# One transfer over 128 partitions in place of two of 64, in a gated convolution and MLP kernel

## The chip, the cores and the metric

The kernel runs on one core of a Trainium2 chip. The metric is the device time of one execution, in microseconds (us). A profiled execution gives a page and a trace, in which the engines are PE (TensorE), DVE (VectorE), ACT (ScalarE), POOL (GpSimd) and SP (SyncE, which here issues nearly all DMAs).

## The reference

2048 rows of 640 channels go through two branches, which a gate mixes row by row.

```python
x = A_q                                        # [1, 2048, 640], bfloat16
g = sigmoid((x * gate_w).sum(-1, keepdims=True))
# branch A: short convolution of k, product with v, long convolution along the rows
kv = conv4(A_k, A_shift_k) * A_v
y  = long_conv(kv, A_ssm_k) + kv * A_ssm_D     # by FFT of length 4096 along the rows
a  = x * y
# branch B: an MLP whose hidden channels are shifted by +1, -1, +2, -2 rows, and a second MLP
h  = gelu(layernorm(x) @ w1)
x1 = x + shift(h) @ w2
b  = x1 + gelu(layernorm(x1) @ w3) @ w4        # w3: 640 x 1536
out = g * a + (1 - g) * b
```

## The kernel before

**Layout of the rows.** A row number is split as 32n + 16g + s, with n from 0 to 63, g (the group) 0 or 1 and s from 0 to 15. Row (n, g, s) lies on partition 64g + n, in slot s of that partition. So one partition holds 16 slots of 640 bfloat16 values (1280 bytes), and in DRAM consecutive n of one group are 32 rows apart, while the two groups are 16 rows apart. The helper `tok` makes the DRAM view:

```python
def tok(ap):
    return ap.rearrange("(n g s) c -> g n s c", g=2, s=16)
```

**Moving rows.** x, k, v, a second reading of q and the output are moved in chunks of two or four slots of all 128 partitions. Since the view has the group as its first index, the kernel uses a helper, `halves` (L377 to L383; its issues stand as L382 in the profile), which issues two transfers one behind the other on SP's queue, of 64 partitions each, group 1 first:

```python
def fn(t):
    for g in (1, 0):
        nc.sync.dma_start(out=out(t, g), in_=in_(t, g))
```

It is called for x (`ldx`, 2 or 4 slots, tile `x`), for k (`ldk`, 4 slots, tile `K`), for v (`ldv`, 4 slots, tile `VC`), for q (`ldq`, 2 slots, tile `QO`) and for the first 12 slots of the output (`st`, 2 slots, from tile `QO`). The last four slots of the output (L1059) are stored slot by slot, half on SP's queue and half on ACT's. Weights, the spectra on their way through DRAM (`FH`, `FXD`, `GD` and back by `FX`, `GX`) and the transposed activations (`x1nT`, `XB`, by DMA transpose, L808) are moved by transfers of their own.

**Order.** The program is a list of tasks whose order is written out by hand (`ORDER`); each engine runs its tasks in that order, and so does SP's queue. A planner (`Plan.place`) turns that list into buffers. A transfer waits on SP's queue until its data or its buffer is ready, and for the transfer eight before it, whose semaphore it takes over.

**Stages.** First x comes in slot by slot (`ldx`), is normalised, transposed and multiplied with w1 (PE L689, L693). Then the products with w2 follow (PE L715), with the first step of the transform of the filter (PE L911) between them. Meanwhile DVE makes kv in four groups `gi` of four slots, from 3 to 0: four products (L878) and three sums (L882), then one product with v (L886, `fin`). There is one buffer for v, so that `ldv` of a group waits for the `fin` of the group before. The first step of the transform of kv (PE L913) writes `FXD`; after all of it `FX` is read back, and PE runs the second step (L965), the product of spectra (DVE L980) and the way back (L993) beside w3 (L817) and w4 (L833). At the end the last step (PE L1031) is scaled by gate and q (DVE L1037), the MLP branch is added (L1064, or L1045 and L1051 for the last four slots), and the output is stored. There are two buffers for q and two for the output, of two slots each.

Of the kernel before, what the change touches and what calls it, by code (L numbers as in the profile page):

```python
# [16 lines left out]
P = 128  # L17
D = 640
# [7 lines left out]
HALF = 1.27  # L26
# [328 lines left out]
def build(env, nc, io):  # L355
    pl = Plan()
    add = pl.add
# [3 lines left out]
    BF = 2  # L361
# [6 lines left out]
    if io:  # L368
# [4 lines left out]
        qv, kv_, vv, ov = tok(q2), tok(k2), tok(v2), tok(o2)  # L373
# [1 line left out]
    def dma(name, nbytes, fn, issue=0.58, **kw):  # L375
        return add(name, "SP", issue, fn, nbytes=nbytes, **kw)

    def halves(name, nbytes, out, in_, **kw):

        def fn(t):  # L380
            for g in (1, 0):
                nc.sync.dma_start(out=out(t, g), in_=in_(t, g))  # L382
        return add(name, "SP", 1.08, fn, nbytes=nbytes, **kw)  # L383

    def copy(t, out, in_):
        if t.on == "ACT":
# [26 lines left out]
    def c_ones(t):  # L413
# [6 lines left out]
        w=[("K", "z")], roles=("K",))  # L420
# [80 lines left out]
    def c_bm(t):  # L501
        for g in range(2):
# [8 lines left out]
                                                  in_=io["sk"].rearrange("d j -> (d j)").unsqueeze(0)), w=["CJR"], roles=("VC",))  # L511
# [25 lines left out]


    for s0, n in ((2, 2), (4, 2), (6, 4), (0, 2), (14, 2), (10, 4)):
        halves(f"ldx{s0}", P * n * D * BF * (HALF if n < 4 else 1.05), lambda t, g, s0=s0, n=n: env["x"][64 * g:64 * g + 64, s0:s0 + n, :],  # L540
               lambda t, g, s0=s0, n=n: qv[g, :, s0:s0 + n, :], w=[("x", s, g) for s in range(s0, s0 + n) for g in range(2)])
    dma("ldw1", 819200, lambda t: nc.sync.dma_start(out=env["W12"][:, 0], in_=io["w1"].rearrange("(t p) n -> p t n", p=P)),
        w=["W1"], roles=("W12",))
    dma("ldw2a", 655360, lambda t: nc.sync.dma_start(out=env["W12"][:, 1, 0:4, :],
# [7 lines left out]
        dma(f"ldsk{cb}", 524288, lambda t, cb=cb: nc.sync.dma_start(out=env["SK"][:, cb, :], in_=io["h"][128 * cb:128 * cb + 128, :]),  # L552
            w=[("SK", cb)], roles=("SK",))
    for i0 in (15, 11, 7, 3):
        halves(f"ldk{i0}", P * 4 * D * BF * 1.05, lambda t, g, i0=i0: env["K"][64 * g:64 * g + 64, i0:i0 + 4, :],
               lambda t, g, i0=i0: kv_[g, :, i0 - 3:i0 + 1, :], w=[("K", i, g) for i in range(i0, i0 + 4) for g in range(2)], roles=("K",))
    dma("ldkh1", 64 * 3 * D * BF * HALF, lambda t: nc.sync.dma_start(out=env["K"][64:128, 0:3, :], in_=kv_[0, :, 13:16, :]),
        w=[("K", i, 1) for i in range(3)], roles=("K",))

# [308 lines left out]


    for gi in (3, 2, 1, 0):  # L870
        halves(f"ldv{gi}", P * 4 * D * BF * 1.05, lambda t, g: env["VC"][64 * g:64 * g + 64, 0, :, :],
               lambda t, g, gi=gi: vv[g, :, 4 * gi:4 * gi + 4, :], w=["V"], roles=("VC",))
        a = 4 * gi

        def tap(t, j, o, a=a):
            VC = env["VC"]
            w = VC[:, 3, j:j + 1, :].broadcast_to([P, 4, D])
            nc.vector.tensor_tensor(out=VC[:, o], in0=env["K"][:, a + 3 - j:a + 7 - j, :], in1=w, op=ALU.mult)  # L878

        def acc(t):  # L880
            VC = env["VC"]
            nc.vector.tensor_tensor(out=VC[:, 1], in0=VC[:, 1], in1=VC[:, 2], op=ALU.add)  # L882

        def fin(t, a=a):
            VC = env["VC"]
            nc.vector.tensor_tensor(out=env["K"][:, a + 3:a + 7, :], in0=VC[:, 1], in1=VC[:, 0], op=ALU.mult)  # L886
        for j in (3, 2, 1, 0):
            rk = [("K", i, g) for i in range(a + 3 - j, a + 7 - j) for g in range(2)] + ([("K", "z")] if a + 3 - j < 3 else [])
            add(f"kv{gi}.m{j}", "DVE", 1.485, lambda t, j=j, a=a: tap(t, j, 1 if j == 3 else 2, a), r=rk + [("CJ", j)],
                w=["VA" if j == 3 else "VB"], roles=("K", "VC"))  # L890
            if j < 3:
                add(f"kv{gi}.a{j}", "DVE", 1.485, acc, r=["VB"], w=["VA"], roles=("VC",))
        add(f"kv{gi}.v", "DVE", 1.49, fin, r=["VA", "V"], w=[("K", i, g) for i in range(a + 3, a + 7) for g in range(2)] +
            [("kv", s) for s in range(a, a + 4)], roles=("K", "VC"))
# [121 lines left out]
    for s0 in range(0, 16, 2):  # L1016
        def rg(t, s0=s0):
            src = env.G.rearrange("k (x n) c -> (k x) (n c)", n=32)[:, 1280 * s0:1280 * s0 + 2560]
            nc.sync.dma_start(out=env["GX"][:, t.buf["GX"][0], :], in_=src)
        ld = dma(f"rG.{s0}", P * 5120, rg, issue=0.5, r=[("G", m) for m in range(10)], acq=("GX",), after=("FX",))  # L1020
        qown = halves(f"ldq.{s0}", P * 2 * D * BF * 1.3, lambda t, g: env["QO"][64 * g:64 * g + 64, 2 * t.buf["Q"][0]:2 * t.buf["Q"][0] + 2, :],
                      lambda t, g, s0=s0: qv[g, :, s0:s0 + 2, :], acq=("Q",), w=[("q", s0)], after=("W12",))
        oown = None
        for i in range(2):
            s = s0 + i

            def mm(t, s=s, i=i, ld=ld):
                X = env["GX"][:, ld.buf["GX"][0], :]
                for (c0, c1) in ((0, 512), (512, 640)):
                    for g in range(2):  # L1030
                        nc.tensor.matmul(env.Uf(t.buf["U"][0])[64 * g:64 * g + 64, c0:c1], lhsT=env["BT"][:, s, 64 * g:64 * g + 64],  # L1031
                                         rhs=X[:, 1280 * i + 640 * g + c0:1280 * i + 640 * g + c1], start=True, stop=True)
            t = add(f"s4.{s}", "PE", 0.29, mm, use=[ld], r=["BT"], rel=[(ld, "GX")], acq=("U",), mode="c64")

            def yq(t_, s=s, i=i, q=qown, t=t):
                u = env["W4"][:, 12 + t_.buf["V"][0], :]
                nc.vector.scalar_tensor_tensor(out=u, in0=env.Uf(t.buf["U"][0])[:, 0:D], scalar=SS("GG")[:, s:s + 1],  # L1037
                                               in1=env["QO"][:, 2 * q.buf["Q"][0] + i, :], op0=ALU.mult, op1=ALU.mult)
            y = add(f"yq.{s}", "DVE", 0.88, yq, use=[t], rel=[(t, "U"), (qown, "Q")], r=["GG", ("q", s0)], acq=("V",),
                    after=("C0",))  # L1040

            if s in LATE:
                def ax(t_, s=s, y=y):
                    u = env["W4"][:, 12 + y.buf["V"][0], :]
                    nc.vector.scalar_tensor_tensor(out=u, in0=env["x"][:, s, :], scalar=SS("OG")[:, s:s + 1], in1=u, op0=ALU.mult, op1=ALU.add)  # L1045
                a = add(f"ax.{s}", "DVE", 0.88, ax, use=[y], r=["GG", ("x", s, 0), ("x", s, 1)])
                for n, (c0, c1) in enumerate(((0, 512), (512, 640))):
                    w = late[s, n]

                    def fo(t_, s=s, i=i, y=y, o=oown, w=w, c0=c0, c1=c1):  # L1050
                        nc.vector.scalar_tensor_tensor(out=env["QO"][:, 4 + 2 * (o or t_).buf["O"][0] + i, c0:c1],  # L1051
                                                       in0=env.PS[:, w.buf["U"][0], 0:c1 - c0], scalar=SS("OG")[:, s:s + 1],
                                                       in1=env["W4"][:, 12 + y.buf["V"][0], c0:c1], op0=ALU.mult, op1=ALU.add)
                    o = add(f"fo.{s}.{n}", "DVE", (0.74, 0.27)[n], fo, use=[a, w] + ([oown] if oown else []), rel=[(y, "V"), (w, "U")],
                            w=[("o", s, n)], after=("W12",), **(dict(acq=("O",)) if oown is None else {}))
                    oown = oown or o
                def st(t, s=s, o=oown, i=i):
                    for g, q in ((1, nc.sync), (0, nc.scalar)):
                        q.dma_start(out=ov[g, :, s, :], in_=env["QO"][64 * g:64 * g + 64, 4 + 2 * o.buf["O"][0] + i, :])  # L1059
                add(f"st.{s}", "SP", 0.58, st, nbytes=P * D * BF * 1.3, r=[("o", s, 0), ("o", s, 1)], rel=[(oown, "O")])  # L1060
                continue

            def ad(t_, s=s, i=i, y=y, o=oown):
                nc.vector.scalar_tensor_tensor(out=env["QO"][:, 4 + 2 * (o or t_).buf["O"][0] + i, :], in0=env["x"][:, s, :],  # L1064
                                               scalar=SS("OG")[:, s:s + 1], in1=env["W4"][:, 12 + y.buf["V"][0], :], op0=ALU.mult, op1=ALU.add)
            kw = dict(acq=("O",)) if oown is None else {}
            o = add(f"ad.{s}", "DVE", 0.88, ad, use=[y] + ([oown] if oown else []), rel=[(y, "V")], r=["GG", ("x", s, 0), ("x", s, 1)],
                    w=[("o", s)], after=("W12",), **kw)
            oown = oown or o
        if s0 in LATE:  # L1070
            continue
        halves(f"st.{s0}", P * 2 * D * BF * 1.3, lambda t, g, s0=s0: ov[g, :, s0:s0 + 2, :],
               lambda t, g, o=oown: env["QO"][64 * g:64 * g + 64, 4 + 2 * o.buf["O"][0]:6 + 2 * o.buf["O"][0], :],
               r=[("o", s0), ("o", s0 + 1)], rel=[(oown, "O")])
    pl.close()
    return pl
# [30 lines left out]
```

## Time and profile before

| | |
|---|---|
| median of 3 runs | 225.56 us (224.49 to 228.49) |
| profiled execution, its own time | 227.05 us |
| its span, first to last instruction | 225.3 us |
| PE busy | 212.7 us (94%) |
| DVE busy | 189.3 us (84%) |
| ACT busy | 154.4 us (69%) |
| moved by DMA | 57.94 MB, mean 257 GB/s |

Busy times are unions over the span. A DMA view lists the issues by tile: how many, how many KB each (1 KB is 1024 bytes), and the median time from issue to landing. A view by windows gives, for a stretch of time, each engine's busy time, the granted clock of PE, the busy share of the core's 16 DMA engines and what they moved in GB/s (10^9 bytes). The chain is the work that ended last, followed back from the last instruction to what released each step.

### The profile page before, as it was taken

How to read it: one execution, taken by the hardware profiler on the slowest of the kernel's cores; microseconds unless marked ns; L12 is line 12 of the kernel's file. 1: busy time of each engine (PE TensorE's matmuls, PEld its weight loads, DVE VectorE, ACT ScalarE, POOL GpSimd, SP SyncE). 2: the span in 40 equal slices, each digit the busy share in tenths (PEclk: the TensorE clock that was granted, in tenths of full speed). 3: DMA queues.
4: the chain of work that ended last, by engine and by line, in shares of the span. 5: the costliest groups of instructions: out<-in, count | busy, mean ns of one | idle time of the engine just before them, and what ended most of it. 6: DMA issues, size and time to landing. Idle time of an engine off the chain costs nothing.

```text
span 225.3 us, 5381 instructions
## 1 busy us (share of the span) xinstructions
PE 212.7 (94%) x2161; PEld 106.4 (47%) x2178; DVE 189.3 (84%) x281; ACT 154.4 (69%) x225; POOL 45.8 (20%) x86
## 2 busy tenths in 40 slices
PE   3999889899999999999999999999999999999992
PEld 1576454466444444345543433334444555555561
DVE  7998896999999999997469989899857426989984
ACT  6998969799988999889658988888675002225000
POOL 7481532436200009930710000000000000000000
PEclk9999999999999999999999999999999999999999
DMA  6999999999999998979899989999992596988624
GB/s 193 281 308 232 220 237 238 327 233 327 349 240 287 241 272 252 379 270 270 193 367 311 373 154 285 316 304 309 247 255 88 185 374 209 281 250 249 203 64 116
DMA packets 39503, 57.94 MB, mean 257 GB/s; under 512 B 15027, under 2 KB 30645, under 8 KB 39478
## 3 DMA queue, kind: packets, MB, share of 16 engines
q1 hardware_dynamic: 39158, 57.27, 89.9%
q10 hardware_dynamic: 320, 0.33, 0.5%
q8 instruction: 17, 0.28, 0.5%
q14 instruction: 8, 0.07, 0.1%
HBM read 35.56 MB, written 18.36 MB: 239 GB/s over the span
## 4 chain that ended last, share of the span: by engine, by line
PE 63%; DMA 17%; DVE 12%; SPq 3%; issue 2%; ACT 1%; DVEq 0%
PE PS L817 18%; PE PS L833 17%; PE PS L715 9%; DMA x<-in_A_q_dram 7%; PE PS L965 5%; DMA W<-in_B_w_dram 4%; PE PS L689 4%; PE PS L993 4%; DMA SK<-in_A_ssm_k_dram 3%; DVE VC L878 3%; DVE VC L882 3%; DMA QO<-in_A_q_dram 2%; SPq L382 2%; PE PS L911 2%; PE PS L1031 1%
## 5 line engine op out<-in xcount | busy, mean ns | idle before, releaser
L824 ACT ACTIVATE h2T<-PS 128x512 bf16<-128x512 f32 x48 | 27.9, 605 | 27.3 <-PE PS L817 26.9
L833 PE MATMUL PS<-W,h2T 128*128 128x512 bf16 (+3 forms) x306 | 39.8, 298 | 0.3
L387 ACT CAST FS<-PS 128x1024 bf16<-128x1024 f32 x37 | 36.0, 1021 | 5.4 <-PE PS L913 3.5
L817 PEld LDWEIGHTS <-W 128*128 128x128 bf16 (+1 forms) x300 | 22.1, 103 | 29.4 <-issue 8.4
L833 PEld LDWEIGHTS <-h2T 128*128 128x128 bf16 (+1 forms) x312 | 22.4, 100 | 18.5 <-issue 1.6
L387 ACT CAST XH<-PS 128x1024 bf16<-128x1024 f32 x26 | 25.5, 1020 | 7.5 <-PE PS L965 7.4
L817 PE MATMUL PS<-x1nT,W 128*128 128x512 bf16 x120 | 28.5, 380 | 0.0
L817 PE MATMUL PS<-XB,W 128*64 128x512 bf16 (+1 forms) x180 | 28.5, 380 | 0.0
L980 DVE TENSOR_TENSOR PP<-XH 128x2048 bf16<-128x2048 bf16 x20 | 23.6, 1219 | 3.1 <-ACT XH L387 2.8
L878 DVE TENSOR_TENSOR VC<-K,VC 128x2560 bf16<-128x2560 bf16 x16 | 23.7, 1490 | 2.3 <-DMA W<-in_B_w_dram 2.1
L715 PE MATMUL PS<-W,hsT 128*128 128x128 bf16 (+1 forms) x155 | 23.5, 297 | 0.9 <-DMA W<-in_B_w_dram 0.6
L850 DVE TENSOR_TENSOR x<-PS,x 128x640 bf16<-128x640 f32 x12 | 9.8, 823 | 13.4 <-PE PS L833 13.2
L689 PE MATMUL PS<-xnT,W 128*128 128x512 bf16 x80 | 19.2, 379 | 0.1
L715 PEld LDWEIGHTS <-hsT 128*128 128x128 bf16 x160 | 12.8, 98 | 13.0 <-issue 1.1
L882 DVE TENSOR_TENSOR VC<-VC 128x2560 bf16<-128x2560 bf16 x12 | 17.9, 1489 | 0.3
L389 DVE CAST XH<-PS 128x1024 bf16<-128x1024 f32 x14 | 16.9, 1220 | 1.2 <-PE PS L965 1.1
L1037 DVE SCALAR_TENSOR_TENSOR W<-PS,GG,QO 128x640 bf16<-128x640 f32 x16 | 13.6, 877 | 2.4 <-PE PS L1031 1.9
L387 ACT CAST GS<-PS 128x1024 bf16<-128x1024 f32 x12 | 12.0, 1016 | 3.9 <-PE PS L993 3.9
L255 PE MATMUL PS<-C 128*128 128x512 bf16 x34 | 9.9, 434 | 3.8 <-DVE C L506 3.7
L842 PE MATMUL PS<-W,h2T 128*64 128x512 bf16 (+1 forms) x192 | 13.4, 299 | 0.0
L722 DVE SCALAR_TENSOR_TENSOR x<-PS,x 128x640 bf16<-128x640 f32 x16 | 12.8, 815 | 0.1
L965 PE MATMUL PS<-FX,TRIG 64*32 64x512 bf16 x320 | 12.4, 381 | 0.3 <-ACT GS L387 0.3
(115 smaller groups left out, 294.0 us busy)
## 6 DMA issues: line engine op xcount, KB each, us to landing
FH<-FS SPq DMA_DIRECT2D x8, 640.0 KB, 6.3
FXD<-FS SPq DMA_DIRECT2D x8, 640.0 KB, 5.0
FX<-FH SPq DMA_DIRECT2D x10, 512.0 KB, 6.0
FX<-FXD SPq DMA_DIRECT2D x10, 512.0 KB, 5.3
GX<-GD SPq DMA_DIRECT2D x8, 640.0 KB, 5.9
W<-in_B_w_dram SPq DMA_DIRECT2D x2, 1920.0 KB, 11.9
GD<-GS SPq DMA_DIRECT2D x8, 480.0 KB, 4.0
SK<-in_A_ssm_k_dram SPq DMA_DIRECT2D x5, 512.0 KB, 6.5
```

The costliest lines, as they stand in the source:

```text
L387: nc.scalar.copy(out=out, in_=in_)
L389: (nc.vector if t.on == "DVE" else nc.gpsimd).tensor_copy(out=out, in_=in_)
L689: nc.tensor.matmul(m[:, b, :], lhsT=W[:, 0, kb, 160 * fb:160 * fb + 128], rhs=rhs(kb, shifts[fb]), start=(kb == 0), stop=(kb == 4))
L715: nc.tensor.matmul(m[:, c0:c1], lhsT=env["hsT"][:, o.buf["hs"][0], fb, 128 * (s % 4):128 * (s % 4) + 128], rhs=env["W12"][:, 1, fb, c0:c1] ...
L817: nc.tensor.matmul(env.PS[q:q + w, t.buf["U"][0], :], lhsT=env["W3"][:, kb, 128 * fb + q:128 * fb + q + w], rhs=env.nT(int(nP[-1]))[:, :, ...
L824: nc.scalar.activation(out=env["h2T"][:, o.buf["h2"][0], fb, :], in_=env.PS[:, t.buf["U"][0], :], func=ACT.Gelu_apprx_tanh)
L833: nc.tensor.matmul(m[q:q + w, c0:c1], lhsT=env["h2T"][:, o.buf["h2"][0], fb, a:a + w], rhs=env["W4"][:, fb, c0:c1], start=(fb == 0), stop= ...
L878: nc.vector.tensor_tensor(out=VC[:, o], in0=env["K"][:, a + 3 - j:a + 7 - j, :], in1=w, op=ALU.mult)
L882: nc.vector.tensor_tensor(out=VC[:, 1], in0=VC[:, 1], in1=VC[:, 2], op=ALU.add)
L965: nc.tensor.matmul(env.U(t.buf["U"][0])[32 * j:32 * j + 32, gp, :], lhsT=CRI()[64 * gp:64 * gp + 64, 32 * pc:32 * pc + 32], rhs=X[64 * gp: ...
L980: nc.vector.tensor_tensor(out=env["PP"][:, o.buf["PP"][0], a, :].rearrange("p (b c) -> p b c", b=2), in0=X.unsqueeze(1).broadcast_to([P, 2 ...
L1037: nc.vector.scalar_tensor_tensor(out=u, in0=env.Uf(t.buf["U"][0])[:, 0:D], scalar=SS("GG")[:, s:s + 1], in1=env["QO"][:, 2 * q.buf["Q"][0] ...
```

## The change

`halves` goes, and `whole` takes its place: one transfer over all 128 partitions, with both groups in one access pattern. The calls, the sizes, the order and everything else stay. The planner's notes on bytes change with it.

```diff
-    def halves(name, nbytes, out, in_, **kw):
-
-        def fn(t):
-            for g in (1, 0):
-                nc.sync.dma_start(out=out(t, g), in_=in_(t, g))
-        return add(name, "SP", 1.08, fn, nbytes=nbytes, **kw)
+    def whole(name, nbytes, out, in_, **kw):
+
+        return add(name, "SP", 0.58, lambda t: nc.sync.dma_start(out=out(t), in_=in_(t)), nbytes=nbytes, **kw)
...
-        halves(f"ldx{s0}", P * n * D * BF * (HALF if n < 4 else 1.05), lambda t, g, s0=s0, n=n: env["x"][64 * g:64 * g + 64, s0:s0 + n, :],
-               lambda t, g, s0=s0, n=n: qv[g, :, s0:s0 + n, :], w=[...])
+        whole(f"ldx{s0}", P * n * D * BF, lambda t, s0=s0, n=n: env["x"][:, s0:s0 + n, :], lambda t, s0=s0, n=n: qv[:, :, s0:s0 + n, :], w=[...])
...
```

The same edit is made to `ldk`, `ldv`, `ldq` and `st`. In the built program the DRAM side of a call on x with two slots was `[[20480, 64], [1, 1280]]` (step and count, slowest first, in elements) for each of the two transfers. It is now `[[10240, 2], [20480, 64], [1, 1280]]` for the one, against an SBUF side of `[[10240, 128], [1, 1], [1, 1280]]`: the 128 partitions are one dimension in SBUF, but in DRAM the two groups and the 64 rows of a group can't be merged into one step.

More of the change, by code (lines that the diff above doesn't have):

```diff
@@ L539, in build @@
     for s0, n in ((2, 2), (4, 2), (6, 4), (0, 2), (14, 2), (10, 4)):
-        halves(f"ldx{s0}", P * n * D * BF * (HALF if n < 4 else 1.05), lambda t, g, s0=s0, n=n: env["x"][64 * g:64 * g + 64, s0:s0 + n, :],
-               lambda t, g, s0=s0, n=n: qv[g, :, s0:s0 + n, :], w=[("x", s, g) for s in range(s0, s0 + n) for g in range(2)])
+        whole(f"ldx{s0}", P * n * D * BF, lambda t, s0=s0, n=n: env["x"][:, s0:s0 + n, :], lambda t, s0=s0, n=n: qv[:, :, s0:s0 + n, :], w=[("x", s, g) for s in range(s0, s0 + n) for g in range(2)])
     dma("ldw1", 819200, lambda t: nc.sync.dma_start(out=env["W12"][:, 0], in_=io["w1"].rearrange("(t p) n -> p t n", p=P)),
@@ L554, in build @@
     for i0 in (15, 11, 7, 3):
-        halves(f"ldk{i0}", P * 4 * D * BF * 1.05, lambda t, g, i0=i0: env["K"][64 * g:64 * g + 64, i0:i0 + 4, :],
-               lambda t, g, i0=i0: kv_[g, :, i0 - 3:i0 + 1, :], w=[("K", i, g) for i in range(i0, i0 + 4) for g in range(2)], roles=("K",))
+        whole(f"ldk{i0}", P * 4 * D * BF, lambda t, i0=i0: env["K"][:, i0:i0 + 4, :], lambda t, i0=i0: kv_[:, :, i0 - 3:i0 + 1, :], w=[("K", i, g) for i in range(i0, i0 + 4) for g in range(2)], roles=("K",))
     dma("ldkh1", 64 * 3 * D * BF * HALF, lambda t: nc.sync.dma_start(out=env["K"][64:128, 0:3, :], in_=kv_[0, :, 13:16, :]),
@@ L870, in build @@
     for gi in (3, 2, 1, 0):
-        halves(f"ldv{gi}", P * 4 * D * BF * 1.05, lambda t, g: env["VC"][64 * g:64 * g + 64, 0, :, :],
-               lambda t, g, gi=gi: vv[g, :, 4 * gi:4 * gi + 4, :], w=["V"], roles=("VC",))
+        whole(f"ldv{gi}", P * 4 * D * BF, lambda t: env["VC"][:, 0, :, :], lambda t, gi=gi: vv[:, :, 4 * gi:4 * gi + 4, :], w=["V"], roles=("VC",))
         a = 4 * gi
@@ L1020, in build @@
         ld = dma(f"rG.{s0}", P * 5120, rg, issue=0.5, r=[("G", m) for m in range(10)], acq=("GX",), after=("FX",))
-        qown = halves(f"ldq.{s0}", P * 2 * D * BF * 1.3, lambda t, g: env["QO"][64 * g:64 * g + 64, 2 * t.buf["Q"][0]:2 * t.buf["Q"][0] + 2, :],
-                      lambda t, g, s0=s0: qv[g, :, s0:s0 + 2, :], acq=("Q",), w=[("q", s0)], after=("W12",))
+        qown = whole(f"ldq.{s0}", P * 2 * D * BF, lambda t: env["QO"][:, 2 * t.buf["Q"][0]:2 * t.buf["Q"][0] + 2, :],
+                    lambda t, s0=s0: qv[:, :, s0:s0 + 2, :], acq=("Q",), w=[("q", s0)], after=("W12",))
         oown = None
@@ L1071, in build @@
             continue
-        halves(f"st.{s0}", P * 2 * D * BF * 1.3, lambda t, g, s0=s0: ov[g, :, s0:s0 + 2, :],
-               lambda t, g, o=oown: env["QO"][64 * g:64 * g + 64, 4 + 2 * o.buf["O"][0]:6 + 2 * o.buf["O"][0], :],
+        whole(f"st.{s0}", P * 2 * D * BF, lambda t, s0=s0: ov[:, :, s0:s0 + 2, :],
+             lambda t, o=oown: env["QO"][:, 4 + 2 * o.buf["O"][0]:6 + 2 * o.buf["O"][0], :],
                r=[("o", s0), ("o", s0 + 1)], rel=[(oown, "O")])
```

## The prediction

> **What bounds the kernel now.** I read the page first (span and chain), then the chain in order of time, then the DMA view, and last the windows that show what one DMA engine can carry.
>
> ```profile
> span 225.3 us, 5381 instructions
> ...
> PE 63%; DMA 17%; DVE 12%; SPq 3%; issue 2%; ACT 1%; DVEq 0%
> ...
> 8.29 6.95 DMA SK<-in_A_ssm_k_dram
> 15.25 15.68 DMA x<-in_A_q_dram
> 30.95 9.63 DMA W<-in_B_w_dram
> 40.63 1.75 PE PS L715 x11
> ```
>
> PE carries 63% of the chain. The 17% of DMA lie mostly in the head: from 8 to 40.6 us the chain runs through SK, the last x and w2, because SP's queue hands them out in that order and each waits behind the one before. At 40.63 PE gets w2 and is nearly always busy from there on. So a transfer that takes longer counts at once in the head; later it counts when it is longer than the work that covers it. The sizes, from the DMA view:
>
> ```profile
> FH<-FS SPq DMA_DIRECT2D x8, 640.0 KB, 6.3
> FXD<-FS SPq DMA_DIRECT2D x8, 640.0 KB, 5.0
> ...
> GX<-GD SPq DMA_DIRECT2D x8, 640.0 KB, 5.9
> W<-in_B_w_dram SPq DMA_DIRECT2D x2, 1920.0 KB, 11.9
> ...
> SK<-in_A_ssm_k_dram SPq DMA_DIRECT2D x5, 512.0 KB, 6.5
> K<-in_A_k_dram SPq DMA_DIRECT2D x8, 320.0 KB, 9.5
> VC<-in_A_v_dram SPq DMA_DIRECT2D x8, 320.0 KB, 6.6
> QO<-in_A_q_dram SPq DMA_DIRECT2D x16, 160.0 KB, 5.5
> out_dram<-QO SPq DMA_DIRECT2D x12, 160.0 KB, 3.4
> x<-in_A_q_dram SPq DMA_DIRECT2D x8, 160.0 KB, 3.3
> x<-in_A_q_dram SPq DMA_DIRECT2D x4, 320.0 KB, 13.9
> ...
> W<-in_B_w_dram SPq DMA_DIRECT2D x1, 800.0 KB
> VC<-CD SPq DMA_DIRECT2D x1, 640.0 KB
> W<-in_B_w_dram SPq DMA_DIRECT2D x1, 640.0 KB, 9.6
> C<-TRIG SPq DMA_DIRECT2D x2, 256.0 KB
> out_dram<-QO SPq DMA_DIRECT2D x4, 80.0 KB, 2.1
> ```
>
> The rows that change are K, VC, x, QO and the 160 KB stores: 56 transfers become 28 of twice the size.
>
> **What the edit removes.** 28 issues on SP's queue, at the median of the L382 rows:
>
> ```profile
> L382 SPq DMA_DIRECT2D x<-in_A_q_dram x12: 471/594/1355, 1.2 to 15.3; - x12
> ```
>
> 28 x 0.594 = 16.6 us of SP, of which little is on the chain: four issues of x ahead of the second SK (2.4 us), and one of QO near the end (0.6 us). That is a gain of 3 us at most, if nothing else changes.
>
> **What it adds.** The new pattern in DRAM has 2 as its slowest dimension, against 128 in SBUF; it had 64 against 64. A transfer has to be cut into shares for the 16 DMA engines, and I take the cut to run along the slowest dimension. Then the old transfers had 16 shares of 4 rows, and the new ones have two shares of 64 rows, which leave 14 engines out. The old rows fit the first half of this: two engines would need 163,840 bytes / 51 GB/s (twice the rate found below) = 3.2 us for the data of a 160 KB load of x alone, and it lands 3.3 us after its issue, 2 of which an 80 KB store needs too (2.1 us). No transfer of the kernel before begins with a dimension of 2, so the trace has no direct price for the second half.
>
> The Trainium skill, page "DMA: Bandwidth & Descriptors", section "Why a DMA increments its semaphore by 16 and not by 1", states it as a rule: the queue takes the largest count of engines up to 16 that divides the slowest dimension (other than one) of both sides, and on this kind of queue the lowest-numbered ones. By it 2 and 128 give two engines, the same two each time. No run here shows it yet. The same page, "Rules for kernel authors", speaks for the change instead: two transfers to disjoint partition halves share the same engines, so one of 128 partitions should be used. By that sentence alone the time would be that of the second rival below.
>
> **Price of one engine.** The windows:
>
> ```profile
> core 0: us, PE busy (x) PEld busy (x) DVE busy (x) ACT busy (x) POOL busy (x), PEclk, DMA share, GB/s
> 2.00:5.00 3.00, 1.27 (x4) 0.45 (x5) 2.79 (x10) 1.67 (x3) 2.92 (x5) 1.00 0.88 294
> 24.00:28.00 4.00, 3.10 (x25) 1.64 (x23) 3.21 (x12) 3.97 (x8) 2.24 (x6) 1.00 1.02 219
> 182.00:185.00 3.00, 3.00 (x24) 1.72 (x23) 0.82 (x1) 0.00 (x0) 0.00 (x0) 1.00 1.01 415
> ```
>
> In 182 to 185 us only GX is read, in rows of 5120 bytes, and every engine carries 415/16 = 25.9 GB/s. In 2 to 5 us (x among others) it is 294/16/0.88 = 20.9, and in 24 to 28 us (x and k, all engines full) 219/16 = 13.7. Two engines ask for some 50 GB/s of a memory that gave 415, so I take a value near the best row, 25 GB/s = 24.4 KB/us. A two-slot transfer (320 KB, 160 a share) then takes 6.55 us and a four-slot one (640 KB) 13.1 us. If the two engines are the same each time, and each works in order, everything behind on SP's queue has its sixteenth behind them too. So the two engines' load, bytes on two engines / 2 plus all other bytes / 16, sets the time wherever they are never idle.
>
> **Head, to w2.** On two engines: all of x (2560 KB) and the first two chunks of k (1280). On sixteen: SK 2560, w1 800, TRIG 512, CD 640, w2 640 and its four small parts of 40: 5312 KB. Load 1920 + 332 = 2252 KB, 92.2 us. With 2 us before the first packets it ends at 94.2. An 80 KB store lands 2.1 us after an issue of 0.5, so I add 1.5 for landing: PE gets w2 at 95.7 instead of 40.6.
>
> **The kv stretch.** The next rows on SP's queue are FH, k, v, k, FH, w3, and the v of the second group. Its anchors on DVE and PE:
>
> ```profile
> 67.15 1.49 DVE L886 TENSOR_TENSOR K<-VC 128x2560 bf16<-128x2560 bf16 x1
> ...
> 96.30 1.49 DVE L886 TENSOR_TENSOR K<-VC 128x2560 bf16<-128x2560 bf16 x1
> ...
> 114.47 0.56 PE PS L965 x16
> ...
> L808 SPq DMA_TRANSPOSE x1nT<-xn x8: 1206/1301/1937, 61.1 to 125.7; - x8
> ```
>
> Two chunks of k and two of v (1280 KB on shares) and 4956 KB on sixteen (four FH 2560, w3 1920, the halo of k 476) load 1590 KB: 65.1 us, to 159.3. Landing 1.5 and `fin` (L886) 1.5 give 162.3, where it ended at 68.6. v has one buffer, so the next v follows: four FH and two transposes (160 KB each) ahead of it load 180 KB (7.4 us), a transpose holds SP's queue 1.3 to 1.9 us, say 1.5 of gap, then 13.1 of v: 181.3. The last: two transposes and three FXD, 140 KB (5.7 us), 1.5, 13.1: 201.6, and `fin` ends at 204.6 in place of 97.8. **The last kv is 106.8 us late.** PE's work of 40.6 to 98 us fits into 95.7 to 204.6 and costs nothing more.
>
> **The middle.** From FX on (PE L965 from 114.5) PE sets the pace and no changed transfer is needed until q. The first two loads of q hold the two engines for 13.1 us, which FX, read ahead into five buffers, covers but for about 1 us. If it didn't, the cost would be up to 13.
>
> **The end.** On the clock of before:
>
> ```profile
> 189.62 1.12 SPq L382 DMA_DIRECT2D QO<-in_A_q_dram  x2
> ...
> L1051 DVE SCALAR_TENSOR_TENSOR QO<-PS,OG,W 128x512 bf16<-128x512 f32 (+1 forms) x8 | 3.8, 542 | 0.1
> ...
> 219.85 2.56 SPq L1059 DMA_DIRECT2D out_dram<-QO  x4
> ```
>
> From 189.6 on six loads of q, six stores and three GX are still to come: 12 x 6.55 + 120 KB / 24.4 = 83.5 us. With two buffers for each, the next load or store is always queued before the last one is through, so the two engines end at 273.1. The last pair of slots waits for the buffer of the last such store: landing 1.5, half of L1051's 3.8, the last store 2.1, and 1.3 to the end, as it is now (219.85 + 2.56 - 0.5 + 2.1 = 224.0 of 225.3): 279.9. **54.6 us late.**
>
> **Sum.** 106.8 + 1 + 54.6 = 162.4 us. The profiled execution has a span of 225.3 and a time of 227.05, 1.75 around it: 389.5. It lies 1.5 above the median of the runs, so on the median it is 225.56 + 162.4 = **388 us**. The 3 us of saved issues are inside the head's load and gain nothing. At 25.9 GB/s the 280 us of load in the sum (92.2 + 65.1 + 20.5 + 18.8 + 83.5) shrink by 10: 378. At 20.9 they grow by 55: 443. At 13.7 by 231: 619.
>
> **The rivals.**
> *Two engines, but other ones each time.* For it: nothing in the trace tells which engines serve a transfer. Then loads run beside each other, the bytes stay spread, and only what waits for a single transfer pays. A load of v lands after 13.1 + 2 instead of 6.6 us, so a kv group takes 16.6 us from one `fin` to the next: from 57.3 (the issue of the second v), 3 x 16.6 = 107 against 97.8, 9 us. At the end a load of q lands 3 later than the 5.5 of its row and the last paired store 5 later. Sum 17 to 18: 243 us.
> *The spread stays at sixteen, and the edit only saves issues* (not slower). It decides if the queue cuts by rows or by the 128 of the SBUF side. Then the 3 us of issues on the chain are its worth: 222 us. Against it is the pattern itself, in which the 2 can't be merged.
> *Two engines at the rate of full contention*, 13.7 GB/s: 619 us. Against it: with 14 engines mostly idle there is little to contend with.
>
> **How the numbers follow.** The forecast (the same two engines, 20.9 to 25.9 GB/s) has 0.85, other engines each time 0.06, no loss of spread 0.07, contention 0.02. The forecast's own range is 378 to 443; its small terms (gaps on SP's queue, cover that fails) can add or take some 20, and a fifth is to be left out over all cases, so the range is 350 to 465. A measurement here tells about 2% from no change, and 222 is 1.6% under 225.56: faster 0.02, same 0.05, slower 0.93.
>
> **What would show it.** Right: the slices of DMA's busy share fall to one or two tenths while x, k, v or q move, and GB/s there to about 50; a 320 KB load of x or q lands 6.5 us or more after its issue, alone; PE's first L715 starts near 96 us and waits for DMA; DVE waits for VC ahead of L886 three times; the chain is mostly DMA and SP's queue; from FX to GX (about 70 us) PE is as dense as now. Wrong: 400 GB/s slices or landings of 4 us on the new x rows mean the spread is kept; a head that ends near 45 us with landings of 7 us means other engines each time. If the head fits and the end does not, the buffers of q and the output left gaps that I did not count.

## The result, and the profile after

The changed kernel takes 400.16 us in the median of 4 runs (398.67 to 400.25), against 225.78 (224.49 to 228.49, 4 runs) for the kernel before: 1.774 times as long, 95% interval 1.765 to 1.783. The ratios and the losses below leave out executions that ran over 1.5% longer than the fastest of the same kernel, as the one of 228.49 us did (the other three have a median of 225.56). The prediction was 388 (350 to 465). The profiled execution took 398.67 us, with a span of 396.7.

First the page of the changed kernel: the span, PE's busy time, three of the rows in 40 slices (9.9 us each), and the chain by engine.

```profile
span 396.7 us, 5351 instructions
...
PE 245.6 (62%) x2179; PEld 120.1 (30%) x2179; DVE 189.7 (48%) x281; ACT 155.7 (39%) x225; POOL 37.1 (9%) x86
...
PEclk9965988755998559677999999987999978558867
DMA  2185113144121479697859999697937413122112
GB/s 83 52 233 162 54 52 104 54 122 169 66 111 53 140 269 65 227 76 266 232 184 208 346 299 228 200 224 209 238 121 276 149 53 109 52 77 86 52 53 88
...
DMA 55%; PE 29%; SPq 7%; DVE 4%; ACT 3%; POOL 1%; issue 1%; DVEq 0%; POOLq 0%; ACTq 0%
```

The chain has turned over: PE had 63% of it and has 29%, DMA had 17% and has 55%. Yet the DMA engines are not busy: in many slices the share is one or two tenths and they move 52 to 54 GB/s. In the kernel before, nearly every slice had nine tenths:

```profile
DMA  6999999999999998979899989999992596988624
```

The windows of the changed kernel show how sharp this is, in two stretches where almost only x is moved (5 to 12 us, and 40 to 66 us, with k already waiting behind it) and in one with q and the output:

```profile
core 0: us, PE busy (x) PEld busy (x) DVE busy (x) ACT busy (x) POOL busy (x), PEclk, DMA share, GB/s
5.00:12.00 7.00, 3.69 (x17) 1.39 (x16) 2.38 (x12) 3.15 (x6) 0.29 (x1) 1.00 0.13 50
...
40.00:66.00 26.00, 17.12 (x150) 9.78 (x149) 11.24 (x27) 10.68 (x15) 4.17 (x7) 0.93 0.13 54
...
340.00:350.00 10.00, 3.94 (x22) 1.83 (x23) 3.36 (x4) 0.60 (x1) 0.00 (x0) 0.50 0.13 51
```

0.13 of 16 engines is 2/16, and 50 to 54 GB/s are 25 to 27 GB/s for each of the two. The Trainium skill, page "DMA: Bandwidth & Descriptors", section "Why a DMA increments its semaphore by 16 and not by 1", gives two engines for a slowest dimension of 2; by these windows the trace agrees.

The chain of the changed kernel in order of time (start, us, what), the pieces that matter:

```profile
7.83 24.64 DMA x<-in_A_q_dram
...
39.25 27.19 DMA CD<-VC
66.84 11.85 SPq L544
78.74 19.15 DMA W<-in_B_w_dram
97.94 4.43 PE PS L710 x20
...
164.82 17.37 DMA VC<-in_A_v_dram
182.28 1.50 DVE K L880
183.80 19.38 DMA VC<-in_A_v_dram
...
203.63 1.49 DVE K L880
...
222.97 0.56 PE PS L959 x16
...
254.36 13.61 DMA FX<-FXD
...
304.76 0.66 PE PS L1025 x8
...
309.60 15.35 DMA QO<-in_A_q_dram
...
334.05 17.92 DMA QO<-in_A_q_dram
...
355.12 17.32 DMA out_dram<-QO
...
374.23 17.24 DMA out_dram<-QO
```

CD is a row of 5 KB, w2 is 640 KB; neither was changed, and they take 27.19 us (10.99 of them are CD's issue on SP's queue) and 19.15 us. CD waits behind x and w2 behind k, on the engines that serve those, too. That these are the same two each time can be read from the trace's records of landings: of the 16 shares of w2, fourteen have landed by 84.3 us, and the last two land at 97.5 and 97.9, just after the second load of k (94.5). With this chain go the waits (us in total, times, longest) of the changed kernel:

```profile
DVE K L880 <- DMA VC<-in_A_v_dram: 38.1, 4, 24.0
...
DVE W L1031 <- DMA QO<-in_A_q_dram: 35.4, 6, 11.1
...
PEld L710 <- DMA W<-in_B_w_dram: 21.2, 1, 21.2
...
PE PS L959 <- DMA FX<-FXD: 7.3, 1, 7.3
```

The span can be cut at four anchors. These rows give the first and the last start of each, in the changed kernel and then, for the one anchor whose row the prediction does not show, in the kernel before:

```profile
L710 PE MATMUL PS<-W,hsT x160: 219/345/634, 97.9 to 207.6; 128*128 128x512 bf16 x80, 128*128 128x128 bf16 x80
L880 DVE TENSOR_TENSOR K<-VC x4: 1491/1492/1493, 127.1 to 203.6; 128x2560 bf16<-128x2560 bf16 x4
L959 PE MATMUL PS<-FX,TRIG x320: 373/386/631, 222.9 to 286.9; 64*32 64x512 bf16 x160
L1025 PE MATMUL PS<-GX,BT x64: 219/346/637, 304.7 to 367.2; 128*64 128x512 bf16 x32, 128*64 128x128 bf16 x32
```

```profile
L1031 PE MATMUL PS<-GX,BT x64: 219/299/403, 187.1 to 212.8; 128*64 128x512 bf16 x32, 128*64 128x128 bf16 x32
```

| stretch | before | after | later by |
|---|---|---|---|
| start to first FX | 114.4 | 222.9 | 108.5 |
| first FX to first GX | 72.7 | 81.8 | 9.1 |
| first GX to the end | 38.2 | 92.0 | 53.8 |
| span | 225.3 | 396.7 | 171.4 |

One thing the prediction had not seen is on SP's queue. Its rows for the changed transfers (ns min/median/max of one issue, first and last start) in the changed kernel:

```profile
L380 SPq DMA_DIRECT2D QO<-in_A_q_dram x8: 526/624/6614, 249.5 to 355.9; - x8
L380 SPq DMA_DIRECT2D x<-in_A_q_dram x6: 536/2853/6048, 1.2 to 37.4; - x6
...
L380 SPq DMA_DIRECT2D K<-in_A_k_dram x4: 557/5954/11482, 50.3 to 99.1; - x4
```

An issue of k takes 6 us in the median and up to 11.5, and every issue behind it waits. So while the two engines work off their queue, SP often can't hand work to the 14 others. The 11.85 us of L544 in the chain are of that kind: it is the issue of a 40 KB part of w2.

### The profile page after: what moved, and what is told of

Its sections match the earlier page's. It is cut to its first block, busy times and chain, and to the rows that moved or that the text cites. A ratio compares the mean times of both kernels' runs of the same rounds, so it can differ in the third digit from the quotient of the medians.

```text
span 396.7 us, 5351 instructions
## 1 busy us (share of the span) xinstructions
PE 245.6 (62%) x2179; PEld 120.1 (30%) x2179; DVE 189.7 (48%) x281; ACT 155.7 (39%) x225; POOL 37.1 (9%) x86
## 4 chain that ended last, share of the span: by engine, by line
DMA 55%; PE 29%; SPq 7%; DVE 4%; ACT 3%; POOL 1%; issue 1%; DVEq 0%; POOLq 0%; ACTq 0%
DMA VC<-in_A_v_dram 9%; PE PS L828 9%; DMA out_dram<-QO 9%; PE PS L812 8%; DMA QO<-in_A_q_dram 8%; DMA FH<-FS 7%; DMA CD<-VC 7%; DMA x<-in_A_q_dram 6%; DMA W<-in_B_w_dram 5%; DMA FX<-FXD 3%; SPq L544 3%; PE PS L710 3%; PE PS L959 3%; PE PS L987 2%; PE PS L684 2%; SPq L380 1%
## 5 line engine op out<-in xcount | busy, mean ns | idle before, releaser
L710 PE MATMUL PS<-W,hsT 128*128 128x512 bf16 (+1 forms) x160 | 28.0, 333 | 30.2 <-DMA W<-in_B_w_dram 20.7
L812 PE MATMUL PS<-x1nT,W 128*128 128x512 bf16 x120 | 31.6, 411 | 5.8 <-DMA x1nT<-xn 5.8
L812 PE MATMUL PS<-XB,W 128*64 128x512 bf16 (+1 forms) x180 | 31.3, 415 | 3.6 <-DVE W L1031 3.6
L905 PE MATMUL PS<-HT,C 128*128 128x512 bf16 (+1 forms) x64 | 13.0, 330 | 31.9 <-ACT FS L384 29.7
L1031 DVE SCALAR_TENSOR_TENSOR W<-PS,GG,QO 128x640 bf16<-128x640 f32 x16 | 13.6, 879 | 36.1 <-DMA QO<-in_A_q_dram 35.4
L880 DVE TENSOR_TENSOR K<-VC 128x2560 bf16<-128x2560 bf16 x4 | 6.0, 1492 | 38.1 <-DMA VC<-in_A_v_dram 38.1
L1025 PE MATMUL PS<-GX,BT 128*64 128x512 bf16 (+1 forms) x64 | 8.0, 374 | 26.1 <-DMA GX<-GD 17.4
L837 PE MATMUL PS<-W,h2T 128*64 128x512 bf16 (+1 forms) x192 | 19.2, 382 | 7.5 <-DVE W L1031 7.5
L684 PE MATMUL PS<-xnT,W 128*128 128x512 bf16 x80 | 23.2, 437 | 0.0
L572 DVE BATCH_NORM_STATS2 BS<-x 128x6 f32<-128x512 bf16 x10 | 6.9, 690 | 33.5 <-DMA x<-in_A_q_dram 33.5
L580 ACT ACTIVATE JK<-x 128x640 bf16<-128x640 bf16 x6 | 4.4, 735 | 35.5 <-DMA x<-in_A_q_dram 35.5
L959 PE MATMUL PS<-FX,TRIG 64*32 64x512 bf16 x320 | 12.8, 393 | 7.6 <-DMA FX<-FXD 7.3
```

The source lines that it names most:

```text
L684: nc.tensor.matmul(m[:, b, :], lhsT=W[:, 0, kb, 160 * fb:160 * fb + 128], rhs=rhs(kb, shifts[fb]), start=(kb == 0), stop=(kb == 4))
L710: nc.tensor.matmul(m[:, c0:c1], lhsT=env["hsT"][:, o.buf["hs"][0], fb, 128 * (s % 4):128 * (s % 4) + 128], rhs=env["W12"][:, 1, fb, c0:c1] ...
L812: nc.tensor.matmul(env.PS[q:q + w, t.buf["U"][0], :], lhsT=env["W3"][:, kb, 128 * fb + q:128 * fb + q + w], rhs=env.nT(int(nP[-1]))[:, :, ...
L837: nc.tensor.matmul(env.PS[q:q + w, t.buf["U"][0], 0:c1 - c0], lhsT=env["h2T"][:, o.buf["h2"][0], fb, a:a + w], rhs=env["W4"][:, fb, c0:c1] ...
L959: nc.tensor.matmul(env.U(t.buf["U"][0])[32 * j:32 * j + 32, gp, :], lhsT=CRI()[64 * gp:64 * gp + 64, 32 * pc:32 * pc + 32], rhs=X[64 * gp: ...
```

## The experiments

The theory: the slowest dimension of the DRAM pattern, 2, puts each changed transfer on two engines, and always on the same two, so that everything behind on the queue waits too. Its rivals: the third dimension or the size of a transfer costs the time; the loss is in single landings, on engines that change from transfer to transfer; SP's issues are the cost.

### The same transfers with the 128 partitions outermost

The rows are cut in their plain order, so that partition and row have one common stride and the pattern has one dimension less. The calls for k, v, q and the output change in the same way. Number, size and order of the transfers stay.

```diff
+qw, kw_, vw, ow = (ap.rearrange("(p s) c -> p s c", s=16) for ap in (q2, k2, v2, o2))
-  ... lambda t, s0=s0, n=n: qv[:, :, s0:s0 + n, :], ...
+  ... lambda t, s0=s0, n=n: qw[:, s0:s0 + n, :], ...
```

> One transfer over 128 partitions, same bytes, sizes and order as in the changed kernel, but the DRAM rows are taken in plain order (partition p reads rows 16p to 16p + 15), so that the pattern is 128 by 1280 (or 2560) with 128 as its slowest dimension. The rows land on other partitions than the reference has them, so the output is not the reference's. Theory (the slowest dimension of 2 leaves two of the 16 DMA engines): spread over 16 again, 28 issues fewer than before, 222 us (219 to 226). Rival (a transfer of twice the size, for which all its readers must wait, is slow in itself): about 400 us, as the changed kernel.

224.68 us (10 runs) against 225.49 (19), ratio 0.997 (0.9945 to 0.9996). From the page and the DMA view of this kernel (the last column is the median us from issue to landing), and its SP row for k:

```profile
PE 214.3 (96%) x2179; PEld 107.4 (48%) x2179; DVE 189.6 (85%) x281; ACT 154.5 (69%) x225; POOL 46.9 (21%) x86
...
K<-in_A_k_dram SPq DMA_DIRECT2D x4, 640.0 KB, 7.2
QO<-in_A_q_dram SPq DMA_DIRECT2D x8, 320.0 KB, 3.6
...
L381 SPq DMA_DIRECT2D K<-in_A_k_dram x4: 332/472/1269, 18.6 to 41.2; - x4
```

So neither the doubled size nor the halved number costs anything: 640 KB of k land in 7.2 us, where half as much took 9.5 before. Its issue takes 0.47 us again, so the 6 us above are not the price of a 128-partition issue. And 28 saved issues with faster landings are worth 0.8 us, little more than the noise; PE is busy for 96% of the span, which leaves little to gain. What the changed kernel loses is all in its pattern.

### A slowest dimension of 16, and of 4

```diff
+qw, kw_, vw, ow = (ap.rearrange("(b a s) c -> a b s c", a=16, s=16) for ap in (q2, k2, v2, o2))
```

and the same with `a=4`; used as in the kernel above. The number of dimensions is that of the changed kernel.

> As the run with 128, but with a pattern of three dimensions as in the changed kernel, whose slowest is 16 instead of 2 (16 by 8 by the row; partition 8a + b reads rows 16(16b + a) on, so the output is not the reference's). Theory: 16 engines with 8 rows each, 223 us (219 to 228). Rival (a third dimension in the pattern, not its count, makes the transfer slow): about 400 us. Rival (size): about 400 us.

> As the run with 16, with 4 as the slowest dimension (partition 32a + b reads rows 16(4b + a) on; the output is not the reference's). Theory: four engines, a four-slot transfer 6.55 us and a two-slot one 3.3 us at 25 GB/s an engine. Head load 960 + 332 KB = 52.9 us, w2 at 56 us instead of 40.6; the last kv about 28 us late; the end 10 to 15 us late: 265 us (250 to 280). DMA moves some 100 GB/s where only these transfers run. Rivals (size, third dimension): about 400 us.

With 16 it is 225.4 us, ratio 0.998 (0.9947 to 1.0022): the third dimension does no harm. With 4 it is 296.16, ratio 1.310 (1.296 to 1.325): in between, and 31 us above what was expected. Two windows of the kernel with 4, the first beside other transfers and the second in a stretch where such transfers run alone, and pieces of its chain:

```profile
5.00:12.00 7.00, 6.75 (x40) 3.28 (x39) 3.08 (x16) 3.99 (x7) 1.62 (x4) 1.00 0.57 157
30.00:40.00 10.00, 10.00 (x92) 6.50 (x90) 6.76 (x19) 7.78 (x10) 1.35 (x3) 1.00 0.26 100
```

```profile
29.39 15.41 DMA CD<-VC
...
46.52 19.09 DMA W<-in_B_w_dram
...
128.38 24.43 DMA W<-in_B_w_dram
```

0.26 is 4/16, and 100 GB/s are 25 for each of four engines: where they run alone, the rate and the count are as expected. The time is not, since the load on the engines at that rate is only a lower bound for it. w2 comes at 65.7 us instead of 56 and the last `fin` starts at 145.9, where I expected its end near 126. CD must land before the read of CD is issued, and everything behind waits on the queue. That the engines run dry in such gaps is not shown: by the packets in the trace, fewer than four are under way for only 1.7 of the 148 us from 2 to 150. A busy engine was slower beside other transfers, 157/16/0.57 = 17 GB/s in 5 to 12 us, which may be a part of it. How the 31 us are made up was not settled.

### One part at a time

`halves` is kept for all but the named calls: x alone, k and v alone, or q and the output alone by 128 partitions.

```diff
-whole(f"ldk{i0}", ...)
+halves(f"ldk{i0}", ...)
...
```

> The kernel before with the new transfer for x alone; k, v, q and the output stay as two of 64. Theory: head load 2560/2 + 6592/16 = 1692 KB, 69.3 us, so w2 reaches PE at 73 us instead of 40.6, and the 32 us stay to the end: 258 us (250 to 268). If the engines were other ones each time, the six loads of x would run beside each other and the head would lose 5 us at most: 226 to 231.

> The kernel before with the new transfer for k and v alone. Theory (two engines, the same each time): the head loads 640 + 7872/16 = 1132 KB, 46 us, so w2 is 5 to 10 us late; then the chain of k and v loads on the two engines and the one buffer for v make the last kv some 60 us late in all: 287 us (275 to 300). If other engines served each load: 9 us for the kv groups, 235 us.

> The kernel before with the new transfer for q and the output alone. Theory: nothing changes until the first two loads of q; these hold back the last reads of FX by 13 us, which the changed kernel's chain shows as a wait of 13.6 and which costs about 9; the end is 54 us late as in the changed kernel: 288 us (278 to 298). If other engines served each load: 8 us at the end, 234 us. With the 40 us of x and 60 of k and v, the three parts would add to 225 + 163 = 388 to 400.

| part | us | before | ratio (95%) | us lost |
|---|---|---|---|---|
| x | 265.27 | 225.49 | 1.174 (1.162 to 1.186) | 39.8 |
| k and v | 297.12 | 226.26 | 1.313 (1.289 to 1.338) | 70.9 |
| q and output | 287.95 | 226.26 | 1.273 (1.251 to 1.294) | 61.7 |

The three losses add to 172.4, and the whole change loses 174.6 (400.16 - 225.56): each part costs its own stretch, and within the noise of some 2 us nothing is paid twice or hidden by another. With x alone, w2 comes at 80.0 us (73 expected); with q and the output alone, the stretch from FX to GX is 194.1 - 112.5 = 81.6 us, so the 9 us in the middle belong to q. That kernel's chain shows the place:

```profile
143.93 13.58 DMA FX<-FXD
```

### The first loads of q by halves again

In the middle, PE (L959) waits 7.3 us for a read of FX that takes 13.6: fourteen of its 16 shares have landed by 260.1 us, the last two at 267.7 and 268.0. Two loads of q stand ahead of it on SP's queue, four-slot work in all, 13.1 us by the prediction; the second lands at 266.7. If these two are the cause, both by halves must give the 9 us back. The diff is that of the first try; the second has `s0 in (2, 6)` in its condition.

```diff
+if s0 < 4:
+    qown = halves(f"ldq.{s0}", ...)
+else:
     qown = whole(f"ldq.{s0}", ...)
```

> The changed kernel with the first two loads of q (slots 0 to 3) as two transfers of 64 partitions again. Theory: the middle loses 9 us because FX waits behind these two loads on the two engines; without them it loses nothing: 391 us (388 to 394), and no wait of PE for FX over 2 us between the first L959 and the first L1025. Rival (the middle is late from something else, such as a slower clock of PE): 400 us.

> The changed kernel with the two loads of q that are issued in the middle (slots 2 and 3, 6 and 7, by the order of the tasks) as two transfers of 64 partitions again; the run q2_halves had hit only one of them and one of the end. Theory: FX waits behind these two on the two engines; without them the stretch from the first L959 to the first L1025 takes 72.7 us as before instead of 81.8, PE waits for FX under 1 us, and the time is 391 us (389 to 393). Rival: the middle is slow from something else too (FX wait of 3 us or more is left): 395 us.

The first try, 389.68 us (ratio 1.722, 1.691 to 1.754), came near its number but was misaimed: of the two loads in the middle it changed only one (slots 2 and 3), and the other (slots 0 and 1) comes at the end. The middle took 300.9 - 223.3 = 77.6 us, with 3.2 of PE's wait left, and the end took 87.3 in place of 92.0. The second try changes the two in question: 390.22 us, ratio 1.728 (1.709 to 1.746). Its anchors:

```profile
L966 PE MATMUL PS<-FX,TRIG x320: 373/376/387, 222.8 to 277.7; 64*32 64x512 bf16 x160
...
L1036 PE MATMUL PS<-GX,BT x64: 218/346/636, 295.5 to 358.7; 128*64 128x512 bf16 x32, 128*64 128x128 bf16 x32
```

295.5 - 222.8 = 72.7 us, as before the change, and PE's wait for FX is gone. So the 9 us are these two loads.

### x from other queues

If the engines were another two for each queue, loads of x from two queues would move at twice the rate. In the first of these kernels all six loads of x come from POOL's queue, in the second three of six (slots 4, 0 and 10) from ACT's; k, v, q and the output go by halves in both.

```diff
+def wholep(...): return add(name, "POOL", 0.58, lambda t: nc.gpsimd.dma_start(...), ...)
...
+wholeq(nc.scalar if s0 in (4, 0, 10) else nc.sync, f"ldx{s0}", ...)
```

> The run with x alone, with the six loads of x issued from POOL's queue instead of SP's; the pattern (2 by 64 by the row) is the same. If a pattern that begins with 2 puts every transfer on the same two engines whatever the queue, the head stays as late as in the run with x alone, 265 us (255 to 275), or a little less as SP's queue is not blocked. If POOL's queue takes other engines for each transfer, the six loads run beside each other: 230 us (226 to 242). The Trainium skill, page DMA: Bandwidth & Descriptors, section Why a DMA increments its semaphore by 16 and not by 1, says the second of this queue (k consecutive engines from a round-robin cursor), and the lowest-numbered k of SP's.

> The run with x alone (265 us), with three of the six loads of x (slots 4, 0 and 10 on) issued from ACT's queue, the others from SP's; the pattern is the same. If both queues use the same two engines, the two engines' load is unchanged and slices where little else runs show 0.13 of the DMA engines busy and 50 GB/s: 262 us (252 to 270; SP's other transfers may pass ACT's). If ACT's transfers get other engines, each pair carries 640 + 412 = 1052 KB, 43 us, and w2 comes at 48 us: 233 us (228 to 244), with 0.25 busy and 100 GB/s.

From POOL's queue: 267.9 us, ratio 1.184 (1.160 to 1.208). The time is that expected for the same two engines, but it tells nothing on them. The loads of x stand behind POOL's own work and come late, and each is slow by itself, as this kernel's chain shows:

```profile
1.42 17.33 DMA x<-in_A_q_dram
...
21.64 9.80 DMA x<-in_A_q_dram
...
35.10 27.78 DMA x<-in_A_q_dram
```

The packets in the trace speak for other engines: from 16 to 22.5 us, with two or three of these loads under way, they move 70 to 76 GB/s by POOL's queue, more than the 50 to 54 that two engines moved above. So "the same two each time" is shown for the queues of SP and ACT, and not for POOL's.

From two queues: 266.57 us, ratio 1.180 (1.161 to 1.200), against 265.27 from one, where two more engines would have given 233. The windows of this kernel, the first with loads of x from both queues outstanding, the second with ACT's last load beside the halves of k on SP's queue:

```profile
5.00:12.00 7.00, 3.73 (x29) 2.12 (x28) 1.46 (x9) 2.56 (x3) 0.29 (x1) 1.00 0.13 52
50.00:60.00 10.00, 0.00 (x0) 0.00 (x0) 0.72 (x2) 0.66 (x2) 0.00 (x0) 0.56 0.13 53
```

0.13 again, and by the packets in the trace each queue has 1.0 under way on average from 8 to 16 us: the second queue shares the same two engines. The page of the Trainium skill named above (same section) says that such a queue takes the lowest-numbered engines, and here the trace agrees in that they are the same; which ones they are was not seen.

## Why the prediction was right, and where not

| step of the prediction | predicted | measured |
|---|---|---|
| rate of one engine, where only such transfers run | 25 GB/s | 25 to 27 |
| w2 at PE | 95.7 us | 97.9 |
| last `fin` ends | 204.6 us | 203.63 + 1.49 = 205.1 |
| FX to GX, later by | 1 us | 9.1 |
| GX to the end, later by | 54.6 us | 53.8 |
| whole span, later by | 162.4 us | 171.4 |

**Right:** the cut along the slowest dimension, shown by four values of one number with the bytes and the order of the transfers kept: 16 and 128 keep the time, 4 costs 31% and 2 costs 77%. Right too is that the engines are the same each time: 0.13 also with the queues of SP and ACT, and 16-share transfers like w2 whose last two shares alone land late. This alone makes the whole queue wait, and the rival of changing engines (243 us) falls with it. The rival that keeps the spread (222 us) falls for the pattern with 2, and is near the truth for the one with 128 (224.68), though the saved issues gained 0.8 us there and not 3. The rate under full contention (619 us) falls by the windows. In the changed kernel no gain of the 3 us of saved issues is seen, as the sum had it.

**Right in sum, but not in mechanism:** the head. The sum had the two engines never idle there. That holds: fewer than two packets are under way for 0.3 us in all between 2 and 98 us, and never from there to 204 us. The head came 2 us late. But it took SP's queue as able to issue ahead, at 0.6 us an issue, and it isn't: L544 holds the chain for 11.85 us. This cost little in the head only because what it delays had to wait for the same two engines anyway, and these had work all the time.

**Mis-sized:** the middle. The step "FX, read ahead into five buffers, covers but for about 1 us" failed. The two loads of q hold their engines for 13.1 us as computed (their packets run from 253 to 266 us); PE then waited 7.3 us for FX at one place, and GX came 9.1 late. The cover was nearer to 4 us than to 12. The 13 was named as the upper end, and the loads by halves have shown that they are the whole cost. This term explains 8 of the 9 us by which the sum fell short.

**Right for the end:** two engines' load, then the last store's landing. In 340 to 350 us only the two are busy, DVE waits 35.4 us for QO ahead of L1031, and the chain is QO and stores to the end. A store takes 17.3 us from issue to landing there, though its bytes are 6.55 us of work: it waits behind the loads and stores issued before it.

Of the signs named, one was wrong: from FX to GX PE is not as dense as before. The others came out (DVE waits for VC four times, not three).

## What to carry to other kernels

Before two transfers are joined into one, write down the pattern of each side with its slowest dimension first: with 2 or 4 there the transfer ran on that many engines and delayed all that was queued behind it, and with 16 or 128 it lost nothing. Counts between these, and counts that don't divide by 16, were not tried. The Trainium skill, page "DMA: Bandwidth & Descriptors", section "Rules for kernel authors", says to prefer one transfer of 128 partitions over two of the halves; here this was worth 0.3% where the partitions were outermost in DRAM as well (224.68 us), and cost 77% where the group was (400.16 us). In a profile, a DMA share that sits at 0.13 or 0.26 while others wait for DMA is the mark of such a transfer.

## What the runs showed of the hardware that was not expected

An issue on SP's queue can itself take long: 6 us in the median and 11.5 at most for k on two engines, 0.47 and 1.27 for the same loads with 128 outermost. It can also hit what stands behind them, as the 10.99 us of CD's issue and the 11.85 of L544's. What limit SP meets there was not tried; the runs show only that it goes with the narrow transfers. Nor was it expected that PE would get a lower clock in a kernel in which it waits: with a mean granted clock of 0.82 (1.00 before) the kernel has PE busy for 245.6 us, where the same matmuls take 214.3 us in the kernel with 128 outermost.
